# Undivided keys and queries for the first two units of an attention and expert kernel

## The chip, the cores and the metric

The kernel runs as one program on 1 core of a Trainium2 chip. The metric is the time of one execution on the device in microseconds (us); the median of several runs is compared. The engines are named as in the profile: PE is TensorE (PEld its weight loads), DVE is VectorE, ACT is ScalarE, POOL is GpSimd, and SP is the engine from whose queue nearly all transfers are issued.

## What is computed

Three layers run one after the other. The first is an attention that keeps, for each query, only the 32 largest scores:

```python
scores = scale * np.matmul(q, k.transpose(0, 1, 3, 2))      # 4 batches, 8 heads, 576 x 576, head_dim 64
kth = np.partition(scores, -top_k, axis=-1)[..., -top_k:-top_k + 1]    # top_k = 32
scores = np.where(scores >= kth, scores, -1e9)
attn = softmax(scores)
attn_out = np.matmul(attn, v)
```

Its output, as 2304 tokens of 512 numbers, goes through a feed-forward layer (`h = max(x @ w_in, 0); h * h @ w_out`, inner width 2048) and then through a layer of 8 experts (inner width 1024) of which a gate picks 2 for each token. All inputs are float32.

## The kernel before

**Division.** A float32 matrix is multiplied as a sum of products of two parts: a rounded one (`fp32r`, made by an ACT copy) and the remainder (a subtraction on DVE or POOL, in `split`, L398 to L401). For keys both parts lie in one tile: the head's 64 rows come twice in the input, rows 0 to 63 of `K4[b, g][:, h]` hold the rounded keys and rows 64 to 127 the remainder. `prep_k` (L403) loads keys into `kn` (2 buffers) and splits them; `prep_q` (L420) loads the queries of one tile and four heads into `qn` (2 buffers) and splits them into `qt[:, 0]` and `qt[:, 1]`. In batch 0 the first keys (`(b, g) == (0, 0)`, heads 0 to 3) come one head at a time and their remainder is made by DVE, as is that of the queries of the first tile; for all later ones it is made by POOL.

**Attention.** The work goes in units: one tile of 128 queries and one pair of heads (`pair_full`, 64 of them), and 16 smaller ones for the left-over 64 queries of each batch (`pair_left`). For each head of a unit `scores` (L429) issues four matmuls into the one `ps` buffer (two halves of the keys, two parts of the queries), ACT copies them to `sb` (L442), and DVE searches `sb`: five pieces of some 115 keys, each with MAX8 (L453) and MATCH_REPLACE8 (L457), and then a `threshold` (L479) that finds the 32nd largest. Its steps are interleaved with the pieces of the next head. The order of the search on DVE is fixed by tokens. Then POOL, ACT, POOL and ACT make the masked exponentials (L506 to L512), PE turns them (L523) and multiplies by the values (L564).

**Beside it.** While units run, `convert` (L144) makes the 32 parts of the feed-forward weights from their stored form: two ACT passes, two DVE passes (L155, L156) and one POOL pass (L158). The first 14 of them hold an intermediate in PSUM (`acc`), the other 18 in SBUF (`ca`). `zero_fill` writes zeros to two buffers in DRAM (`xs`, then `out`) from SP's queue. The feed-forward of tokens that are done is put between the units in small steps (`step`), at a pace that is set by sums of estimated costs; the first of its seven chunks runs in plain float32 (L315, L351).

**Order.** The code is written in the order of the units (L846 on: queries and keys of the first units, their scores, then `prep_k(0, 1, ...)`, values and the loop over units). A scheduler then orders the instructions of each engine by dependences, by priorities (`tc.high_priority`, `tc.cur_priority`) and by its own estimate of the times, so a change of a few instructions can move many others. An engine runs its own instructions strictly in that order.

**Lines that the prediction speaks of:** L400 and L401 (`split`), L409 (loads of keys), L424 (loads of queries), L439 (score matmuls), L442 (their copy), L453 (first search), L155 and L156 (conversion on DVE).

## Time and profile before

| | |
|---|---|
| median of 3 runs | 1337.8 us (1335.57 to 1337.93) |
| the profiled execution | 1336.86 us, of which its span is 1335.1 us |
| PE busy | 1241.5 us (93%) |
| DVE busy | 899.2 us (67%) |
| ACT busy | 856.6 us (64%) |
| POOL busy | 746.2 us (56%) |
| moved by DMA | 270.06 MB, mean 202 GB/s |

The span runs from the first to the last recorded instruction of the core. A busy share over the whole span mixes stages with different limits: the attention stage ends at about 760 us, and the experts fill the rest. So the share says little about one place; the views by stretch, the chain and the timelines do.

### The profile page before, as it was taken

What the parts mean: (1) busy time and instruction counts of PE and PEld (TensorE: products, weight loads), DVE (VectorE), ACT (ScalarE), POOL (GpSimd) and SP (SyncE); (2) the same over time, 40 slices, a digit from 0 to 9 for tenths busy, and PEclk for the clock granted to TensorE, in tenths of its full rate; (3) what the DMA queues carried; (4) which work ended last, traced back from release to release, by engine and by line L of the source; (5) the groups of instructions that cost most, each with busy time, mean ns of one, the idle gap of its engine ahead of it and who ended that gap; (6) DMA issues with size and microseconds to landing.
All of it is one profiled execution on the core that took longest, in us unless ns stands there. A gap on an engine that the chain in (4) does not pass through costs nothing.

```text
span 1335.1 us, 26136 instructions
## 1 busy us (share of the span) xinstructions
PE 1241.5 (93%) x8030; PEld 1071.8 (80%) x8030; DVE 899.2 (67%) x4557; ACT 856.6 (64%) x1886; POOL 746.2 (56%) x1243
## 2 busy tenths in 40 slices
PE   3769889989998999999999999999999999999997
PEld 2556667777887888888888888899899999988886
DVE  8999989998986899978677410255534343444554
ACT  6878879989897889987878653543433333332443
POOL 5857798887786676767655635333432241503221
PEclk9889999999999999999999999999999999999999
DMA  9998886875675554366534689366643443534464
GB/s 333 361 368 292 274 273 235 309 260 181 219 231 193 166 174 157 106 211 204 168 115 158 205 297 332 113 198 197 192 151 117 143 136 119 174 103 143 141 202 140
DMA packets 93302, 270.06 MB, mean 202 GB/s; under 512 B 11612, under 2 KB 11740, under 8 KB 93152
## 3 DMA queue, kind: packets, MB, share of 16 engines
q1 hardware_dynamic: 83872, 239.91, 54.3%
q0 software_dynamic: 9280, 28.40, 5.9%
q8 instruction: 65, 1.06, 0.3%
q14 instruction: 85, 0.70, 0.2%
HBM read 209.90 MB, written 60.45 MB: 202 GB/s over the span
## 4 chain that ended last, share of the span: by engine, by line
PE 61%; ACT 13%; DVE 11%; DMA 7%; issue 5%; POOL 3%; SPq 0%; POOLq 0%; DVEq 0%; ACTq 0%
PE pa L564 5%; PE ph L693 5%; PE ph L695 4%; PE ph L694 4%; PE acc L676 4%; PE acc L674 4%; PE acc L675 4%; PE ps L439 4%; PE pa L523 3%; PE acc L322 3%; PE acc L320 3%; PE acc L321 3%; DMA raww<-in_exp 3%; PE pf L357 2%; PE pf L358 2%
## 5 line engine op out<-in xcount | busy, mean ns | idle before, releaser
L511 POOL TENSOR_TENSOR sb<-sb,w 128x576 f32<-128x576 f32 x144 | 205.8, 1430 | 63.3 <-ACT w L510 59.3
L453 DVE MAX8 m<-sb 128x8 f32<-128x115 f32 (+1 forms) x720 | 190.3, 264 | 53.1 <-ACT sb L442 47.6
L457 DVE MATCH_REPLACE8 w<-m,sb 128x115 f32<-128x115 f32 (+1 forms) x720 | 187.1, 263 | 0.0
L699 ACT ACTIVATE ht<-ph 128x384 fp32r<-128x384 f32 (+1 forms) x128 | 55.8, 436 | 195.2 <-PE ph L695 177.0
L715 POOL DMA_INDIRECT out<-y,info x40 | 45.1, 1127 | 242.4 <-DVE y L714 224.7
L439 PE MATMUL ps<-K,qt 128*128 128x288 f32 (+2 forms) x640 | 131.4, 333 | 43.9 <-ACT sb L442 30.0
L700 DVE SCALAR_TENSOR_TENSOR ht<-ph,ht 128x384 fp32r<-128x384 f32 (+1 forms) x128 | 62.7, 490 | 161.7 <-ACT ht L699 148.5
L693 PE MATMUL ph<-xe,wi 128*128 128x256 f32 (+1 forms) x512 | 159.9, 312 | 1.9 <-ACT wi L686 1.0
L695 PE MATMUL ph<-xe,wi 128*128 128x256 f32 (+1 forms) x512 | 159.2, 311 | 0.2 <-DVE wi L687 0.2
L694 PE MATMUL ph<-xe,wi 128*128 128x256 f32 (+1 forms) x512 | 158.9, 310 | 0.0
L439 PEld LDWEIGHTS ps<-K,qt 128*128 128x128 f32 x640 | 103.7, 204 | 64.4 <-ACT sb L442 37.7
L512 ACT ACTIVATE sb<-sb,keep 128x576 f32<-128x576 f32 x144 | 112.5, 781 | 28.1 <-POOL sb L511 27.6
L674 PE MATMUL acc<-wo,ht 128*128 128x512 f32 x320 | 125.8, 397 | 0.4 <-DVE y L714 0.4
L675 PE MATMUL acc<-wo,ht 128*128 128x512 f32 x320 | 125.3, 395 | 0.0
L510 ACT ACTIVATE w<-sb,keep 128x576 f32<-128x576 f32 x144 | 111.3, 775 | 16.4 <-POOL keep L506 16.2
L371 POOL TENSOR_TENSOR gt<-r,gt 128x384 fp32r<-128x384 f32 (+1 forms) x96 | 90.7, 946 | 53.2 <-ACT gt L370 39.9
L481 DVE MAX8 m<-w 128x8 f32<-128x288 f32 x288 | 116.0, 443 | 0.1
L357 PE MATMUL pf<-xT,wi 128*128 128x384 f32 (+1 forms) x320 | 106.0, 331 | 5.4 <-ACT r L364 3.9
L523 PE MATMUL pa<-ident,sb 128*128 128x128 f32 x576 | 94.8, 289 | 16.5 <-ACT sb L512 7.1
L676 PE MATMUL acc<-wo,ht 128*128 128x512 f32 x320 | 108.9, 401 | 0.0
L525 ACT COPY pt<-pa 128x512 f32<-128x512 f32 x144 | 83.2, 578 | 32.1 <-PE pa L523 21.2
L693 PEld LDWEIGHTS ph<-xe,wi 128*128 128x128 f32 x512 | 96.4, 188 | 8.5 <-ACT wi L686 1.4
(211 smaller groups left out, 3511.9 us busy)
## 6 DMA issues: line engine op xcount, KB each, us to landing
raww<-in_exp SPq DMA_DIRECT2D x88, 512.0 KB
wi<-wsc SPq DMA_DIRECT2D x64, 512.0 KB
wo<-wsc SPq DMA_DIRECT2D x64, 512.0 KB
raw<-in_ffn SPq DMA_DIRECT2D x32, 512.0 KB
xs<-xr SPq DMA_DIRECT2D x40, 258.0 KB
mr<-xs SPq DMA_DIRECT2D x40, 258.0 KB
qn<-in_q SPq DMA_DIRECT2D x40, 256.0 KB
whole<-ca SPq DMA_DIRECT2D x32, 256.0 KB
```

Source lines behind the costliest of these rows:

```text
L357: nc.tensor.matmul(ph[:, 0:n], wi[:, 0, sl], xT[:, 0, c, 0:n], start=(c == 0), stop=False)
L439: nc.tensor.matmul(ps[:, n, 0:w], st, kt[:, at:at + w], start=(i == 0), stop=(i == len(pairs) - 1))
L453: in_turn(nc.vector.max(parts[i][1], sb[:, parts[i][0]]))
L457: in_turn(nc.vector.match_replace(out=w[:, sl], in_to_replace=top, in_values=sb[:, sl], imm_value=NEG))
L511: nc.gpsimd.tensor_tensor(sb, sb, w, op=ALU.subtract)
L523: nc.tensor.transpose(pt[:, c * P:(c + 1) * P], e[:, c * P:(c + 1) * P], ident)
L674: queued(nc.tensor.matmul(acc[t], hs[i][:, 0, sl], wo[:, 0, :], start=(f == 0), stop=False))
L675: queued(nc.tensor.matmul(acc[t], hs[i][:, 0, sl], wo[:, 1, :], start=False, stop=False))
L676: queued(nc.tensor.matmul(acc[t], hs[i][:, 1, sl], wo[:, 0, :], start=False, stop=(f == NFE - 1)))
L693: queued(nc.tensor.matmul(ph[:, 0:n], wi[:, 0, sl], xe[i][:, 0, c, :], start=(c == 0), stop=False))
L694: queued(nc.tensor.matmul(ph[:, 0:n], wi[:, 0, sl], xe[i][:, 1, c, :], start=False, stop=False))
L695: queued(nc.tensor.matmul(ph[:, 0:n], wi[:, 1, sl], xe[i][:, 0, c, :], start=False, stop=(c == NC - 1)))
```

## The change

The first two units (tile 0 of batch 0, heads 0 to 3) take their scores from `kn` and `qn` as loaded, in plain float32: one matmul per half of the keys instead of two, over 64 rows. As the head's rows lie twice in `kn` and `qn`, the first half of the keys uses rows 0 to 63 and the second half rows 64 to 127. The four heads share two `kn` buffers that stay in use until `divide_first`, which is called behind the scores of both units, has split them into `K4[0, 0]` for the later units. The remainders of these keys, and of the other queries of tile 0, are now made by POOL.

```diff
--- before.py
+++ after.py
@@ -404,12 +404,23 @@
 
         if j == 0:
             K4[b, g] = apool.tile([P, 4, S], F32R, name="K4", bufs=3)
-        for h in ([2 * j], [2 * j + 1]) if (b, g) == (0, 0) else ([2 * j, 2 * j + 1],):
-            kn = apool.tile([P, 2, S], F32, name="kn", bufs=2)[:, 0:len(h), :]
-            nc.sync.dma_start(kn, k[b, 4 * g + h[0]:4 * g + h[-1] + 1].rearrange("h p s -> p h s"))
-            dst = K4[b, g][:, h[0]:h[-1] + 1, :]
-            for i in range(len(h)):
-                split(nc.vector if (b, g) == (0, 0) else nc.gpsimd, dst[:, i], dst[:, i], kn[:, i], D)
+        kn = apool.tile([P, 2, S], F32, name="kn", bufs=2)
+        if (b, g) == (0, 0):
+            for i in range(2):
+                nc.sync.dma_start(kn[:, i, :], k[b, 2 * j + i])
+                undivided.append(kn[:, i, :])
+            return
+        nc.sync.dma_start(kn, k[b, 4 * g + 2 * j:4 * g + 2 * j + 2].rearrange("h p s -> p h s"))
+        for i in range(2):
+            dst = K4[b, g][:, 2 * j + i]
+            split(nc.gpsimd, dst, dst, kn[:, i], D)
+
+    undivided = []
+
+    def divide_first(j):
+        for h in (2 * j, 2 * j + 1):
+            dst = K4[0, 0][:, h]
+            split(nc.gpsimd, dst, dst, undivided[h], D)
 
     def prep_v(b):
         V[b] = []
@@ -422,11 +433,13 @@
 
         qn = apool.tile([P, 4, P], F32, name="qn", bufs=2)
         nc.sync.dma_start(qn.rearrange("p h s -> p (h s)"), q[b, s0 // P, g])
+        if (b, g, s0) == (0, 0, 0):
+            return qn
         qt = apool.tile([P, 2, 4, P], F32R, name="qt", bufs=3)
-        split(nc.vector if b == 0 and s0 == 0 else nc.gpsimd, qt[:, 0], qt[:, 1], qn, 0)
+        split(nc.gpsimd, qt[:, 0], qt[:, 1], qn, 0)
         return qt
 
-    def scores(pairs, sb, whole, then):
+    def scores(pairs, sb, whole, then, in_halves=False):
 
 
         ps = ps_s.tile([P, 2, 512], F32, name="ps")
@@ -436,7 +449,9 @@
                     at, w = n * HS, HS
                 else:
                     at, w = ((LEFT * par, NFULL * P), (0 if par else NFULL * P, LEFT))[n]
-                nc.tensor.matmul(ps[:, n, 0:w], st, kt[:, at:at + w], start=(i == 0), stop=(i == len(pairs) - 1))
+                rows = slice(n * D, (n + 1) * D) if in_halves else slice(0, P)
+                nc.tensor.matmul(ps[:, n, 0:w], st[rows], kt[rows, at:at + w], start=(i == 0),
+                                 stop=(i == len(pairs) - 1))
         with tc.high_priority(SOON):
             if whole:
                 nc.scalar.activation(sb.rearrange("p (n s) -> p n s", n=2), ps[:, :, 0:HS], AF.Copy)
@@ -565,17 +580,20 @@
                                              start=(n == 0), stop=(n == NFULL))]
         return av, t5[:, 1, :]
 
-    def pair_full(b, j, qt):
+    def pair_full(b, j, qt, keys=None):
 
         hA = 2 * j
         q0 = 2 * (j % 2)
         sm = apool.tile([P, 2], F32, name="sm", bufs=6)
         e = apool.tile([P, 2 * S], F32, name="sb", bufs=4)
         for i in range(2):
-            kt = K4[b, j // 2][:, (hA + i) % 4]
             sb = e[:, i * S:(i + 1) * S]
-            scores([(qt[:, 0, q0 + i, :], kt, i), (qt[:, 1, q0 + i, :], kt, i)], sb, True,
-                   lambda w, m, sb=sb, one=sm[:, i:i + 1]: softmax(sb, w, m, one))
+            if keys:
+                pairs = [(qt[:, q0 + i, :], keys[hA + i], i)]
+            else:
+                kt = K4[b, j // 2][:, (hA + i) % 4]
+                pairs = [(qt[:, 0, q0 + i, :], kt, i), (qt[:, 1, q0 + i, :], kt, i)]
+            scores(pairs, sb, True, lambda w, m, sb=sb, one=sm[:, i:i + 1]: softmax(sb, w, m, one), bool(keys))
             yield
         recip(sm)
         pts = [transpose4(e)]
@@ -811,6 +829,9 @@
 
     def start(i):
         b, s0, full, j, _ = units[i]
+        if i < 2:
+            gens[i] = pair_full(b, j, qtt[b, s0, j // 2], undivided)
+            return
         gens[i] = (pair_full if full else pair_left)(b, j, qtt[b, s0, j // 2])
 
     def close(i):
@@ -852,6 +873,8 @@
     start(1)
     next(gens[1])
     next(gens[1])
+    divide_first(0)
+    divide_first(1)
     prep_k(0, 1, 0)
     prep_k(0, 1, 1)
     prep_v(0)
```

How this moves instructions, at three places. On ACT at the start of the program (`K_...` is `K4[0, 0]`, `kn` the loaded keys, `sb` the copied scores of a head); before, then with the change:

```order
L400 ACTIVATE qt<-qn 128x512
L400 ACTIVATE K_120<-kn 128x576 x2
L442 ACTIVATE sb<-ps 128x576 x2
L400 ACTIVATE K_120<-kn 128x576 x2
L400 ACTIVATE qt<-qn 128x512 x2
L442 ACTIVATE sb<-ps 128x576
```

```order
L400 ACTIVATE K_117<-kn 128x576 x3
L457 ACTIVATE sb<-ps 128x576
L400 ACTIVATE K_117<-kn 128x576
L457 ACTIVATE sb<-ps 128x576
L400 ACTIVATE qt<-qn 128x512
L457 ACTIVATE sb<-ps 128x576
```

The copy of the first head's scores (L442, now L457) stood behind the query split and the key splits of two heads; it now stands behind the key splits of three heads.

On DVE, from the end of the first head's search on (L453 and L457 are now L468 and L472, L481 is L496, L484 is L499, L489 is L504); before, then with the change:

```order
L457 MATCH_REPLACE w<-m,sb 128x115 x2
L453 MAX m<-sb 128x8
L481 MAX m<-w 128x8 x2
L453 MAX m<-sb 128x8
L401 TENSOR_TENSOR K_120<-kn,K_120 64x576
L484 TENSOR_SCALAR low<-m 128x5x11
L457 MATCH_REPLACE w<-m,sb 128x116
L401 TENSOR_TENSOR K_120<-kn,K_120 64x576
L489 MAX low_164<-low 128x8
L453 MAX m<-sb 128x8
L401 TENSOR_TENSOR qt<-qn,qt 128x512
```

```order
L472 MATCH_REPLACE w<-m,sb 128x115 x2
L468 MAX m<-sb 128x8
L496 MAX m<-w 128x8 x2
L468 MAX m<-sb 128x8
L499 TENSOR_SCALAR low<-m 128x5x11
L472 MATCH_REPLACE w<-m,sb 128x116
L504 MAX low_152<-low 128x8
L468 MAX m<-sb 128x8
```

The three subtractions that stood between the steps of the search are gone from DVE, and three more that stood ahead of its first step.

On SP, which issues the transfers (`kn` keys, `vt` values, `qn` queries, `raw` weights, `xs` zeros); before, then with the change:

```order
L409 DMA kn<-in_k 128x576 x2
L418 DMA vt<-in_v 128x512 x5
L125 DMA wg<-in_route 128x64
L409 DMA kn<-in_k 128x576
L126 DMA nz<-in_noise 128x144
L409 DMA kn<-in_k 128x576
L424 DMA qn<-in_q 128x512 x2
L147 DMA raw<-in_ffn 128x1024 x4
L136 DMA xs<-xr 128x516 x4
L409 DMA kn<-in_k 128x2x576
L136 DMA xs<-xr 128x516
L409 DMA kn<-in_k 128x2x576
```

```order
L147 DMA raw<-in_ffn 128x1024 x4
L413 DMA kn<-in_k 128x2x576
L136 DMA xs<-xr 128x516 x5
L429 DMA vt<-in_v 128x512
L136 DMA xs<-xr 128x516 x2
L435 DMA qn<-in_q 128x512
L429 DMA vt<-in_v 128x512
L136 DMA xs<-xr 128x516 x2
L413 DMA kn<-in_k 128x2x576
```

With the change the four single-head loads stand together behind the first load of queries, ahead of the values. The keys of heads 4 and 5 (the first 128x2x576) now come right behind the four loads of weights; those of heads 6 and 7 (the second) behind nine loads of zeros instead of five.

## Rows read from the trace of the kernel before

**Rows 1.** The view by stretch, the whole core; its columns stand first.

```profile
core 0: us, PE busy (x) PEld busy (x) DVE busy (x) ACT busy (x) POOL busy (x), PEclk, DMA share, GB/s
6.00:7.00 1.00, 1.00 (x4) 0.76 (x4) 0.34 (x1) 0.63 (x1) 0.00 (x0) 1.00 1.07 358
8.00:192.00 184.00, 135.26 (x771) 100.16 (x772) 183.48 (x996) 149.82 (x320) 133.41 (x141) 0.91 0.95 327
192.00:430.00 238.00, 219.07 (x1713) 183.85 (x1712) 205.64 (x1313) 210.89 (x516) 195.35 (x301) 0.99 0.69 234
430.00:760.00 330.00, 322.15 (x2350) 282.70 (x2349) 268.04 (x1794) 272.14 (x618) 225.57 (x365) 1.00 0.50 164
760.00:1335.00 575.00, 563.50 (x3197) 503.91 (x3195) 239.06 (x448) 219.84 (x431) 188.58 (x410) 1.00 0.52 171
```

**Rows 2.** The chain in order of time, first 60 us; start, us, what.

```profile
1.24 3.00 DMA kn<-in_k
...
11.18 0.77 DVE K L401
...
12.24 0.21 issue
...
12.46 0.77 DVE K L401
...
13.64 0.59 DVE qt L401
...
56.58 2.33 PE pa L564 x20
```

**Rows 3.** The timeline of TensorE, first scores; start, us, line, op, count, [idle before <-releaser].

```profile
5.78 1.33 PE L439 MATMUL ps<-K,qt 128*128 128x288 f32 x4 [5.78 <-DVE K L401]
```

**Rows 4.** The timeline of ScalarE, copies and key splits.

```profile
4.26 0.68 ACT L400 ACTIVATE K<-kn 128x576 fp32r<-128x576 f32 x1
...
5.95 0.68 ACT L400 ACTIVATE K<-kn 128x576 fp32r<-128x576 f32 x1 [1.01 <-DMA kn<-in_k]
...
7.15 0.65 ACT L442 ACTIVATE sb<-ps 128x576 f32<-128x576 f32 x1 [0.52 <-PE ps L439]
...
26.38 1.26 ACT L400 ACTIVATE K<-kn 128x576 fp32r<-128x576 f32 x2 [0.94 <-DMA kn<-in_k]
```

**Rows 5.** The timeline of VectorE, first searches of four heads.

```profile
7.83 0.46 DVE L453 MAX8 m<-sb 128x8 f32<-128x116 f32 x2 [0.41 <-ACT sb L442]
...
9.97 0.27 DVE L453 MAX8 m<-sb 128x8 f32<-128x116 f32 x1
...
28.87 0.28 DVE L453 MAX8 m<-sb 128x8 f32<-128x116 f32 x1 [0.26 <-ACT sb L442]
...
36.51 0.27 DVE L453 MAX8 m<-sb 128x8 f32<-128x116 f32 x1
```

**Rows 6.** One line's instructions: plain float32 matmuls of L351; ns min/median/max.

```profile
L351 PE MATMUL pf<-xT,wi x128: 378/380/636, 102.2 to 199.1; 128*128 128x256 f32 x128
```

**Rows 7.** One line's instructions: plain float32 matmuls of L315; ns min/median/max.

```profile
L315 PE MATMUL acc<-wo,gt x64: 591/593/1062, 110.5 to 204.8; 128*128 128x512 f32 x64
```

**Rows 8.** The timeline of POOL, the first splits.

```profile
13.58 1.80 POOL L401 TENSOR_TENSOR qt<-qn,qt 128x512 fp32r<-128x512 f32 x1 [9.44 <-ACT qt L400]
...
26.76 4.16 POOL L401 TENSOR_TENSOR K<-kn,K 64x576 fp32r<-64x576 f32 x3
```

**Rows 9.** The waits of SP's queue, 0 to 60 us; in total, times, longest.

```profile
SPq L136 <- DMA xs<-xr: 9.4, 13, 1.7
```

**Rows 10.** One tile's instructions (ca), 0 to 230 us; ns min/median/max.

```profile
L155 DVE TENSOR_SCALAR ca<-ca x18: 400/590/1564, 112.4 to 180.5; 128x512 uint32<-128x512 uint32 x18
...
L156 DVE SCALAR_TENSOR_TENSOR ca<-raw,ca x18: 664/676/1896, 113.1 to 182.8; 128x512 uint32<-128x512 uint32 x18
```

**Rows 11.** Groups by line and shape, VectorE, 100 to 195 us.

```profile
L156 DVE SCALAR_TENSOR_TENSOR ca<-raw,ca 128x512 uint32<-128x512 uint32 x18 | 18.1, 1007 | 0.0
...
L155 DVE TENSOR_SCALAR ca<-ca 128x512 uint32<-128x512 uint32 x18 | 14.7, 818 | 0.0
```

## The prediction, made before the changed kernel ran

> **What bounds the kernel now.** I read the view by stretch first, to see which engine is full where. From 8 to 192 us DVE is busy for 183.48 of 184 us [rows 1]; PE has 135.26 there, ACT and POOL less than 150. So the search and the weight conversions on DVE set the pace of the first 192 us. From 192 us on PE takes over: 219.07 of 238, then 322.15 of 330, then 563.50 of 575 us [rows 1]. PE's work is fixed, and much of it (the feed-forward of tokens that are done) waits for what DVE has searched; so whatever DVE reaches earlier before 192 us should move the end by as much, and a gain of any other engine there moves nothing.
>
> Then I read the chain at its start, to see what stands ahead of DVE's search. It goes from the load of the first keys (3.00 us from 1.24 us [rows 2]) over ACT's and DVE's split and the score matmuls (5.78 us [rows 3]) to ACT's copy (7.15 us [rows 4]); the search begins at 7.83 us [rows 5] and DVE hardly rests again. Behind that, the chain lies on two key splits and a query split that DVE does in the midst of the search [rows 2].
>
> **Where the search begins.** The first score matmul no longer waits for splits, only for keys and queries: the keys land at 4.24 us (1.24 + 3.00 [rows 2]), so PE could begin some 1.5 us sooner than 5.78. What comes next on the path is not PE but ACT's queue. There the first head's copy now stands behind three key splits, and ACT takes its instructions in order. It can split head 0 at 4.26 and head 1 at 5.95 us, when that load lands [rows 4]. Head 2's load now follows head 1's: 288 KB are 0.295 MB, at 358 GB/s [rows 1] 0.82 us, so it lands at about 6.77. Then one split (0.68) and the copy (0.65 [rows 4]) end at 8.10, and the search begins at 8.12: **0.29 us later than before**. Lower bound: head 2 lands together with head 1, and the search begins at 7.98 (+0.15). Upper: it lands as long behind head 1 as that did behind head 0 (5.95 - 4.24 = 1.71), 7.66, and the search begins at 9.01 (+1.18). I take +0.29, by the rate of the queue at that time.
>
> **The second head.** DVE wants it 2.14 us after the first (9.97 - 7.83 [rows 5]). Its scores can start only when the one score buffer has been copied, so after the first copy come the matmuls (d), a copy of 0.65 and gaps of about 0.07: DVE waits for d - 1.42. Before, d was 1.33 us (four matmuls [rows 3]). Now it is two plain float32 matmuls of 288 columns. One such matmul is two records (128 records of L351 for 64 calls [rows 6]). From 256 to 512 columns a record grows from 636 to 1062 ns at its longest [rows 6, 7], 1.66 ns a column, so 0.48 us for 288. Four records in a row, the last with its tail (636 + 32 x 1.66 = 689 ns), take 3 x 0.48 + 0.69 = 2.13 us, and DVE would wait 0.71. If the two halves of the array work side by side it is 0.48 + 0.69 = 1.17, and no wait. The nearest row is L564: its plain float32 matmuls use half of the array's columns in turn, and 20 records of 128 columns take 2.33 us [rows 2], against 20 x 128 x 1.66 = 4.25 in a row, 0.55 of it. I take **no wait**, and keep 0.71 as the bound.
>
> The Trainium skill, "TensorEngine Tiling (Array Packing)", Key Properties, says that tiles operate independently and can load weights and multiply in parallel. By that rule the wait is nothing, and without it the sum below ends 0.71 us higher. The L564 rows agree for columns; no row of this trace shows row halves.
>
> **What DVE no longer does.** Behind the first search two key splits (0.77 each on the chain) and one query split (0.59) go, 2.13 us, with the gaps beside them (0.21 the largest [rows 2], about 0.28 in all): **2.41 us**. The three splits ahead of the first search were in the path of its start, which is counted above. Lead of DVE at this point: 2.41 - 0.29 = 2.12 us.
>
> **What takes that work.** POOL gets four key splits and a query split: 4 x 1.39 (4.16 for three) + 1.80 [rows 8] = 7.4 us. It was idle for 9.44 us before its first split [rows 8], and nothing on DVE waits for these results until the third unit's tile, so I cost it at nothing; if that cover were gone, the first maskings on POOL would be late by up to 7.4 us, with DVE still ahead in its own order. ACT has the same key splits and one query split less. SP issues as many loads. The loads of heads 2 and 3 now precede the values, so the second unit's keys are there long before the search wants them.
>
> **Units 3 and 4, the divided keys of heads 4 to 7.** They share `kn` with the undivided ones. Heads 4 and 5 now stand ahead of the zeros in the queue and come sooner; before, DVE waited 0.26 us for that unit [rows 5], and I take this wait as gone. Heads 6 and 7 come later. Ahead of their load stood 7794 KB (8 loads of 256 KB, four of 288, four weights of 512, five zeros of 258, the first pair's 576 and its own, 104 KB of small ones); now 9338 KB (10 of 256, nine zeros). The 1544 KB more are 1.58 MB, at 358 GB/s 4.4 us. They landed at 26.38 us [rows 4]; now 30.8. Then ACT's split (0.63) and POOL's (1.4) end at 32.8, four matmuls (1.33 [rows 3]) and the copy (0.65) at 34.8. DVE wanted this head at 36.51 [rows 5]; with the lead it wants it at 36.51 - 2.12 - 0.26 = 34.13. **It waits 0.7 us.** Lower bound: none, if the queue serves the pair out of order. Upper: the load waits behind one more slow block of zeros, for which SP waits up to 1.7 us [rows 9], 2.4 us in all.
>
> **The sum.** 2.12 + 0.26 - 0.7 = 1.7 us ahead after the fourth unit. From there DVE has work without a break to 192 us, and then PE has. So 1336.86 - 1.7 = 1335.2 us for the profiled execution (span 1335.1 plus 1.8 around it), which stands 0.9 us under the median of 1337.8; against the median **1336.1 us**. A measurement of this kernel can tell about 0.2%, 2.7 us, from no change, so this is "the same". With all bounds good the gain is 1.7 + 0.14 + 0.7 = 2.5; with all bad (0.89, 0.71, 1.7 more) the loss is 1.6.
>
> **The rivals.** The scheduler reorders about the first 430 us. The amounts of work between heads are nearly the same, yet the neighbours change, and one place is sensitive to that.
>
> *Fewer collisions (faster).* The 18 conversions that keep their intermediate in SBUF run between 112 and 183 us. Their DVE passes take 400 to 1564 and 664 to 1896 ns [rows 10], and in all 14.7 + 18.1 = 32.8 us [rows 11], where 18 x 0.40 + 18 x 0.664 = 19.2 would be the least. So 13.6 us are lost on DVE, while it is the bound. In the timeline 16 of the 36 passes are longer than their least by over 0.2 us, 0.85 us each. With five fewer stretched the gain is 4.2 more: 1331.9 us. For it: the order there changes, and chance sets who meets whom. The Trainium skill, "SBUF — State Buffer", Who interferes with whom, calls this an exclusive lock between DVE and GpSimd, which the later one to issue waits out; the passes of 1.5 us beside POOL passes of 1.3 us fit that.
>
> *More collisions (slower).* The same mechanism at the same place: two more stretched passes (1.7 us) eat the lead, and from the sixth on the kernel is slower by over 0.2%. With seven more it is 1336.1 + 5.9 = 1342.0 us.
>
> *Late keys (slower).* If heads 6 and 7 land 5 us behind the queue's estimate, DVE waits them out one for one: 1341.1 us. It decides from 4.4 us behind on, a landing at 35.2. Against it: SP's longest wait for a block of zeros in the first 60 us is 1.7 [rows 9], and it takes several in a row.
>
> That the change doesn't do what it says (an early first search) is already in the sum, through ACT's order. Were the copy not held up there, the search would begin 2 us sooner: 1334.1 us. The order of the rows excludes it.
>
> **How the numbers follow.** The forecast, with collisions about as before, 0.40, and all of it within 0.2%. Fewer collisions 0.36, faster. More collisions 0.17, slower. Late keys 0.07, of which 0.05 slower and 0.02 within 0.2%. So faster 0.36, same 0.42, slower 0.22. The forecast's own range is 1335.3 (gain 2.5) to 1339.4. The range of 8 in 10 takes in the collisions on both sides and, since PE idles 18.9 us between 192 and 430 us [rows 1] and a tenth of that may move either way, 1.9 us more: from 1331.9 - 1.9, with the best start 0.5 less, 1329.5, to 1342.0.
>
> **What would show it.** Right: first MAX8 at 8.0 to 9.0 us, behind ACT's third key split; no DVE subtraction of L401; fourth unit's first MAX8 at 34 to 35.5 us with a short wait on ACT's copy; DVE full to about 190 us; conversion passes between 28 and 37 us in all. Wrong: a first MAX8 before 7.8 us, DVE idle for microseconds before the fourth unit, or DVE's lead of the fourth unit lost or doubled before 192 us with the passes unchanged.

## The result, and the profile after

| | before | with the change |
|---|---|---|
| median of the runs | 1336.7 us of 4 (1335.57 to 1337.93) | 1345.88 us of 4 (1341.37 to 1349.33) |
| ratio, 95% interval | | 1.0065 [1.0047, 1.0083] |
| the profiled execution | 1336.86 us, span 1335.1 | 1341.37 us, span 1339.6 |

The kernel is **slower by 0.65%**, some 9 us, where 1336.1 us and a range of 1329.5 to 1342.0 had been predicted. The profiled execution is the fastest of the four and 4.5 us longer than that of before, so it shows about half of the loss.

Lines of the changed kernel: scores L453, their copy L457 (L459 for the left-over units), first search L468, threshold L499 to L509, masking L521 to L527, turning L538 and L565, a broadcast `rb` by POOL L563 and the matmul that wants it L566.

**The first 35 us came out close to the forecast.** The timeline of TensorE with the change, then its first four records by their line (ns min/median/max):

```profile
4.48 1.33 PE L453 MATMUL ps<-kn,qn 64*128 64x288 f32 x4 [4.48 <-DMA kn<-in_k]
...
32.68 1.33 PE L453 MATMUL ps<-K,qt 128*128 128x288 f32 x4 [1.26 <-POOL K L401]
```

```profile
L453 PE MATMUL ps<-kn,qn x4: 684/748/846, 4.5 to 5.1; 64*128 64x288 f32 x4
```

The timelines of ScalarE, VectorE and POOL with the change:

```profile
5.36 1.51 ACT L400 ACTIVATE K<-kn 128x576 fp32r<-128x576 f32 x2 [0.31 <-DMA kn<-in_k]
6.77 0.63 ACT L457 ACTIVATE sb<-ps 128x576 f32<-128x576 f32 x1
...
30.05 1.24 ACT L400 ACTIVATE K<-kn 128x576 fp32r<-128x576 f32 x2
```

```profile
7.43 0.46 DVE L468 MAX8 m<-sb 128x8 f32<-128x116 f32 x2 [4.06 <-ACT sb L457]
...
34.73 0.28 DVE L468 MAX8 m<-sb 128x8 f32<-128x116 f32 x1 [1.03 <-ACT sb L457]
```

```profile
5.19 5.50 POOL L401 TENSOR_TENSOR K<-kn,K 64x576 fp32r<-64x576 f32 x4 [1.06 <-ACT K L400]
...
31.22 2.78 POOL L401 TENSOR_TENSOR K<-kn,K 64x576 fp32r<-64x576 f32 x2 [0.34 <-POOL rb L563]
```

The score matmuls of a head take 1.33 us as before [rows 3]; the first records of the two halves start at 4.481 and 4.488 us, the second ones at 5.090 and 5.129. The first copy stands behind the third key split, as forecast, but the loads were there sooner, so the search begins at 7.43 us and not at 8.12. POOL does the key splits. DVE reaches the fourth unit at 34.73 us after a wait of 1.03; before, that was 36.51 [rows 5]: 1.78 us ahead.

**The loss comes later, in waits for copies.** The view by stretch with the change:

```profile
8.00:192.00 184.00, 135.16 (x758) 97.56 (x756) 177.18 (x978) 149.41 (x321) 137.66 (x148) 0.90 0.93 326
192.00:430.00 238.00, 217.71 (x1695) 184.62 (x1690) 204.95 (x1307) 207.91 (x503) 190.92 (x294) 0.98 0.68 232
430.00:760.00 330.00, 322.16 (x2364) 282.31 (x2364) 270.29 (x1813) 273.48 (x621) 228.32 (x367) 1.00 0.51 165
```

DVE is busy for 177.18 us where it was for 183.48 [rows 1]. Of the 6.3 us only some 2.2 are splits that it no longer does (0.76, 0.76 and 0.68) and 1.8 are shorter conversion passes (below); most of the rest is work that it reaches later (18 instructions fewer here, 19 more from 430 to 760 us). The waits of VectorE from 160 to 212 us, and from 270 to 400 (engine, line, waited for: us in total, times, longest), with the change, and its two longest on the timeline:

```profile
DVE m L468 <- ACT sb L459: 11.3, 2, 5.7
...
DVE m L468 <- ACT sb L457: 14.3, 5, 4.1
```

```profile
189.73 0.28 DVE L468 MAX8 m<-sb 128x8 f32<-128x116 f32 x1 [5.55 <-ACT sb L459]
...
199.63 0.28 DVE L468 MAX8 m<-sb 128x8 f32<-128x116 f32 x1 [5.73 <-ACT sb L459]
```

and the waits before:

```profile
DVE sm L518 <- ACT sm L517: 5.3, 3, 2.5
DVE m L453 <- ACT sb L444: 1.7, 1, 1.7
...
DVE m L453 <- ACT sb L442: 8.2, 5, 2.5
```

How far DVE is ahead can be read head by head: the start of a head's first threshold step (L484 before, L499 now; 144 heads) less its start in the kernel before, in us, negative is ahead. One profiled execution each; e1 to e18 are the experiments below (e10, e13 and e15, not in the table, stand at 6.9, 11.0 and 2.0 us at 440 us).

| head (us before) | change | e1 | e2 | e3 | e4 | e5 | e6 | e11 | e17 | e18 | e7 | e8 | e9 | e12 | e14 | e16 |
|---|---|---|---|---|---|---|---|---|---|---|---|---|---|---|---|---|
| 10 (58) | -1.6 | -0.3 | 3.2 | 1.2 | -1.5 | -1.5 | -0.2 | -1.5 | -0.9 | -1.6 | -0.7 | -0.7 | -0.8 | -0.7 | -1.2 | 0.1 |
| 31 (170) | -1.4 | -0.3 | 5.2 | -1.1 | -3.3 | -2.4 | -1.1 | -1.3 | 0.9 | 0.5 | 0.9 | -1.2 | -0.8 | 0.1 | 0.3 | -0.9 |
| 34 (189) | 2.1 | -0.3 | 8.7 | 0.1 | -2.2 | -2.4 | -1.1 | -1.3 | 0.9 | 0.5 | 4.4 | -1.2 | 5.7 | 2.1 | 3.8 | -0.9 |
| 46 (255) | 1.3 | -1.3 | 8.2 | 0.8 | -0.9 | -2.5 | -0.8 | -2.2 | 1.0 | -0.5 | 4.5 | -1.0 | 7.4 | 9.9 | 3.3 | -1.8 |
| 64 (348) | 7.4 | -1.3 | 18.4 | 4.5 | 2.7 | -2.5 | -0.1 | -2.2 | 1.7 | -0.5 | 4.6 | 4.6 | 7.3 | 10.1 | 10.6 | -1.7 |
| 82 (440) | 4.1 | -1.7 | 15.1 | 2.3 | 3.3 | -2.4 | -0.6 | -0.7 | 0.7 | -1.2 | 4.2 | 2.3 | 6.3 | 9.5 | 7.5 | -1.8 |

The lead of 1.6 us lasts to 170 us, is gone at 189, and DVE falls 7.4 us behind by 348. Some 3 us are made up by 440 us, and from there to 620 us the distance stays at 4.0 to 4.1.

**What stands there.** Of the instructions from the fifth unit to some 430 us that both orders hold (as the lists of e1 and e13 below have them), 259 of 467 on POOL, 507 of 780 on ACT and 788 of 1684 on DVE stand at another place of their queue, by up to 43 places. The copies of two left-over units, with the change and before:

```profile
175.25 0.58 ACT L459 ACTIVATE sb<-ps 128x512 f32<-128x512 f32 x1
...
189.10 0.60 ACT L459 ACTIVATE sb<-ps 128x512 f32<-128x512 f32 x1
```

```profile
172.20 0.60 ACT L444 ACTIVATE sb<-ps 128x512 f32<-128x512 f32 x1 [0.36 <-PE pa L550]
...
186.71 0.60 ACT L444 ACTIVATE sb<-ps 128x512 f32<-128x512 f32 x1
```

They come 3.05 and 2.39 us later than before, while DVE had got 3.8 us ahead just then (head 33); for the second it waits 5.55 us (189.73) and, one unit on, 5.73 (199.63).

**Collisions were not it.** The conversions with an intermediate in SBUF, by the tile's instructions with the change, sum to 14.9 and 16.1 us, 31.0 in all against 32.8 before [rows 11]:

```profile
L155 DVE TENSOR_SCALAR ca<-ca x18: 402/716/1516, 109.3 to 179.2; 128x512 uint32<-128x512 uint32 x18
L156 DVE SCALAR_TENSOR_TENSOR ca<-raw,ca x18: 665/677/1597, 111.2 to 180.4; 128x512 uint32<-128x512 uint32 x18
```

### The profile page after: what moved, and what is told of

It is laid out like the page before. It is cut to its first block, busy times and chain, and to the rows that moved or that the text cites. A ratio compares the mean times of both kernels' runs of the same rounds, so it can differ in the third digit from the quotient of the medians.

```text
span 1339.6 us, 26139 instructions
## 1 busy us (share of the span) xinstructions
PE 1244.7 (93%) x8030; PEld 1073.0 (80%) x8030; DVE 892.0 (67%) x4551; ACT 857.2 (64%) x1885; POOL 753.6 (56%) x1248
## 5 line engine op out<-in xcount | busy, mean ns | idle before, releaser
L468 DVE MAX8 m<-sb 128x8 f32<-128x115 f32 (+1 forms) x720 | 190.9, 265 | 71.9 <-ACT sb L457 56.5
L472 DVE MATCH_REPLACE8 w<-m,sb 128x115 f32<-128x115 f32 (+1 forms) x720 | 187.5, 263 | 0.0
L453 PE MATMUL ps<-K,qt 128*128 128x288 f32 (+1 forms) x624 | 127.9, 330 | 32.5 <-ACT sb L457 25.1
L453 PEld LDWEIGHTS ps<-K,qt 128*128 128x128 f32 x624 | 99.6, 199 | 51.7 <-ACT sb L457 32.0
L527 ACT ACTIVATE sb<-sb,keep 128x576 f32<-128x576 f32 x144 | 112.2, 779 | 29.0 <-POOL sb L526 28.5
L525 ACT ACTIVATE w<-sb,keep 128x576 f32<-128x576 f32 x144 | 111.3, 774 | 20.1 <-POOL keep L521 20.0
L496 DVE MAX8 m<-w 128x8 f32<-128x288 f32 x288 | 116.0, 444 | 0.1
L538 PE MATMUL pa<-ident,sb 128*128 128x128 f32 x576 | 94.4, 288 | 15.4 <-ACT sb L527 7.7
L357 PE MATMUL pf<-xT,wi 128*128 128x384 f32 (+1 forms) x320 | 105.5, 330 | 3.2 <-ACT r L364 3.2
L359 PE MATMUL pf<-xT,wi 128*128 128x384 f32 (+1 forms) x320 | 102.4, 320 | 1.8 <-POOL wi L341 1.8
```

The costliest lines, as they stand in the source:

```text
L453: nc.tensor.matmul(ps[:, n, 0:w], st[rows], kt[rows, at:at + w], start=(i == 0), stop=(i == len(pairs) - 1))
L468: in_turn(nc.vector.max(parts[i][1], sb[:, parts[i][0]]))
L472: in_turn(nc.vector.match_replace(out=w[:, sl], in_to_replace=top, in_values=sb[:, sl], imm_value=NEG))
L496: in_turn(nc.vector.max(m[:, 40 + 8 * i:48 + 8 * i], w[:, i::2]))
L527: nc.scalar.activation(sb, sb, AF.Exp, bias=bs[:, 3:4] if keep is not None else bs[:, 0:1], scale=SCALE, accum_out=sm)
```

## The experiments

Theory: the change gains what was forecast, and the order that the scheduler draws for the other instructions of the first 430 us loses more. Rival: the change costs by itself, through POOL's new work or the later keys.

### Change and order apart (e1, e2)

Each engine got a list of instruction numbers and a dependence without a semaphore from each entry to the next, so that the scheduler keeps that order from the fifth unit to some 430 us:

```diff
+    by_name = {i.name: i for i in nc.cur_bb.bb.instructions}
+    for ids in json.loads(zlib.decompress(base64.b85decode(ORDER))).values():
+        for a, b in zip(ids, ids[1:]):
+            tc.add_manual_dep(by_name[f"I-{b}"], f"I-{a}", ...)
```

e1 is the changed kernel in the old order, e2 the kernel before in the new one.

> The changed kernel, with the order of the kernel before written in by hand (as dependences that only fix the issue order) on all five engines, from the fifth unit on, to past 430 us. Theory O (the change itself gains 1.7 us by the fifth unit; what it loses later comes only from the order that the scheduler redraws from there to 430 us): 1.0 to 2.5 us under the kernel before, about 1335 us, with the lead of VectorE kept to 430 us. Rival C (the change costs by itself, by the splits that POOL now does and the work that it displaces): slower than before by 4 us or more, about as the changed kernel.

> The kernel before, unchanged in its work, with the order of the changed kernel written in on all five engines from the fifth unit on. Theory O: slower than the kernel before by 5 to 11 us (the 4 to 9 that the changed kernel shows, and the lead of 1.7 that it lacks), 1342 to 1348 us. Rival C: within 2.7 us of the kernel before, since its work is unchanged.

e1: 1334.57 us against 1334.81, ratio 1.0001 [0.9987, 1.0015]. e2: 1345.99 us, ratio 1.0081 [1.0056, 1.0105]. **The order alone makes the loss**: with all of the old work and none of the change it costs 0.8%. The two waits at the left-over units are there to the hundredth, as VectorE's timeline of e2 shows:

```profile
196.36 0.28 DVE L609 MAX8 m<-sb 128x8 f32<-128x116 f32 x1 [5.55 <-ACT sb L600]
...
206.27 0.28 DVE L609 MAX8 m<-sb 128x8 f32<-128x116 f32 x1 [5.73 <-ACT sb L600]
```

That a written list costs by itself is excluded by e16 below, the kernel before with its own order as a list and one move: ratio 0.9999 [0.9990, 1.0009]. How large the loss is, is known less well: the same new order gives 0.65% in the changed kernel (4 runs), 0.81 in e2 (4 runs) and 0.39 [0.24, 0.54] in e13 (9 runs, below). The change in the old order costs nothing, but gains nothing that these runs can tell. Why, VectorE's and ScalarE's timelines of e1 show:

```profile
46.53 0.70 DVE L311 TENSOR_SCALAR acc<-acc 128x512 uint32<-128x512 uint32 x1 [1.88 <-ACT acc L309]
```

```profile
41.02 0.78 ACT L681 ACTIVATE w<-sb,keep 128x576 f32<-128x576 f32 x1 [0.87 <-POOL keep L677]
```

POOL, with five more splits ahead, is late with a mask; ACT waits for it, its conversion pass stands behind, and DVE waits 1.88 us for that in the midst of the search. 1.4 of the 1.7 us are gone at 58 us, by this one trace. The old order was drawn for a POOL without these splits.

### Another small edit, another draw (e3, e4)

In e3 (the kernel before) and e4 (the changed one) DVE does the first step of the first two heads twice, some 0.5 us; the second result is dropped.

```diff
+                    for _ in range(1 if i == 0 and not searched[0] and not pending else 0):
+                        in_turn(nc.vector.max(parts[i][1], sb[:, parts[i][0]]))
```

> The kernel before with the first MAX8 of each of the first two heads done twice (the same result; 2 x 0.18 us more on VectorE), which makes the scheduler redraw its order up to about 430 us, as the change does. Theory O: the time moves by several us, in either direction, by far more than the 0.4 us of added work; a move of 2 to 10 us in size. Rival C: 0.4 us slower, within 0.2%.

> The changed kernel with the same two repeated MAX8, and an order redrawn once more. Theory O: the time moves away from that of the changed kernel by several us, in either direction, and may fall below the kernel before. Rival C: 0.4 us over the changed kernel, 6 to 12 us over the kernel before.

e3: 1336.67 us, ratio 1.0015 [1.0002, 1.0028]; e4: 1341.33 us, ratio 1.0045 [1.0028, 1.0061]. In e3's trace, matched by kind and turn, some 280 of POOL's 467 instructions stand at another place because of two added on DVE. Of its 0.15% the work is 0.04. These two runs do not part theory and rival: e3's 1.9 us are fewer than the 2 to 10 of the theory and within the rival's 0.2%, and e4's interval overlaps that of the changed kernel. What the theory rests on is e2. A new draw cost between 0.1 and 0.8% here; none of those seen was better than the old one.

### The new order for 60 us, the old behind (e5)

Two lists can be joined at any time of a run: what an engine had begun by then stands in the one order, the rest in the other. e5 leaves the change its own order to 61 us, made with POOL's splits in view, and takes the old one from there.

> The change; every engine's instructions stand in the order of the changed kernel for its first 61 us and from there in the order of the kernel before. The first run with the old order lost 1.4 us of the lead at 46 us to a wait on ACT; here DVE should be about 1.7 us ahead of the kernel before at 70 us. Theory carried (what DVE gains before 192 us moves the end): the lead stays 1.5 to 1.8 us to the left-over units at 180 us and the end; span 1.4 us under that of the run with the old order, median about 1333.2, ratio to before 0.9988. Rival absorbed (PE and the waits between 192 and 430 us take it up): the lead is there at 170 us and is what the run with the old order had (1.65) or less at 440 us; median about 1334.6, ratio 1.000.

1332.27 us against 1335.25, ratio 0.9986 [0.9972, 1.0000]; span 1330.3 against e1's 1332.3. The lead is 1.5 us at 58 us and 2.4 at 440. This speaks for *carried*: the early lead reaches the end where the order behind does not lose it. It is not shown: the intervals of e1 and e5 overlap, their traces were taken on different chips, and among the runs within 2.5 us the lead of one execution does not order the ratios (at 440 us e1 is 1.7 ahead with a ratio of 1.0001, e11, further down, 0.7 ahead with 0.9984).

### Earlier still (e6, e11)

e6 moves four things in e5's lists:

```diff
 ACT:  key split head 0
+      copy of the first head's scores
       key splits heads 1 to 3
...
       copy of the scores of head 5
+      key splits heads 6, 7
 SP:   load of keys 4, 5
+      load of keys 6, 7
 POOL: product x2
+      key splits heads 6, 7
       query split, mask, rb
```

> As the run beside it, and in the first 60 us three more places are moved by hand: the copy of the first head's scores right behind the first key split on ACT, the load of the keys of heads 6 and 7 right behind that of heads 4 and 5, and their splits ahead of the next query split. First MAX8 at about 6.5 us instead of 7.4, no wait of DVE at the fourth unit's first head (1.03 before): up to 1.9 us more lead at 60 us. Theory carried: the whole of it shows at the end, span 3.3 us under that of the kernel before and below, median 1331.5 to 1333, ratio 0.9975. Rival absorbed: lead of up to 3.6 us at 170 us, no more than 1.7 at the end, ratio 0.9985 to 1.000.

1334.67 us, ratio 1.0001 [0.9990, 1.0012], a miss. The search begins at 6.44 us, but the lead at 58 us is 0.2. TensorE's timeline of e6:

```profile
33.96 0.48 PE L734 MATMUL pa<-ident,rb 128*128 128x128 f32 x1 [2.09 <-POOL rb L731]
34.09 1.31 PE L621 MATMUL ps<-K,qt 128*128 128x288 f32 x4
```

The fourth unit's keys are ready earlier, but its score matmuls stand on PE behind the matmul that wants `rb`, and `rb` now stands on POOL behind the key splits and a query split: PE waits 2.09 us. On ACT the third head's copy (12.45) stands behind a query split that waits 3.22 us for its load. e11 mends both: that copy ahead of that split, and on POOL the mask and `rb` between the two key splits.

> Second try at an earlier start on top of the new order to 60 us and the old behind. The first try lost what it won because ACT's copy of the third head stood behind a query split that waited for its load, and because POOL's key splits held back the broadcast that PE waits for. Here the third head's copy stands ahead of that query split, and on POOL the broadcast stands between the two key splits and the query splits behind them. Theory carried: first MAX8 at 6.4 us, no wait over 0.3 us at the fourth unit's first head, lead over the kernel before of 2.5 to 3.5 us at 70 us (1.76 without these moves), all of it at the end: median 1330.5 to 1331.5 against 1332.3. Rival (another wait takes its place in the first 60 us, as in the first try): lead below 1.8, median 1332.3 or more.

1334.89 us against 1336.98, ratio 0.9984 [0.9972, 0.9996]. The search begins at 6.50 us and the fourth unit has no wait, and yet that unit begins at 34.70, no sooner than with the change alone (34.73): 0.68 us go in a wait at the second head, 0.76 at a normalisation that waits for ACT, and the rest to other work. The lead at 58 us is e5's (at 440 us 0.7 are left of it), and so is the time, within the intervals. So the rival holds for the moves, and e5 and e11 are **the versions that beat both kernels**, by some 0.15%; e11's interval lies wholly below 1, e5's ends there.

### Which stretch of the order (e7, e8, e17, e18)

New order to 250 us and the old behind (e7), the mirror (e8), and the joint of e7 at 118 (e17) and at 160 us (e18):

> The change in its own order to 250 us, from there in the order of the kernel before. DVE is then late by what it lost at 189 us: +0.3 to +1.2 us between 212 and 250 us as in the changed kernel. Theory late order (most of the loss is made by the order between 250 and 430 us, where DVE waits on ACT copies that stand behind late work): no further loss, DVE +0.5 to +1.5 at 440 us, median 1335.5 to 1337, ratio 1.001. Rival early order (what is set up before 250 us makes the loss): DVE +4 at 440 us, median 1341 or more, ratio 1.005.

> The mirror: the change in the order of the kernel before to 250 us, from there in its own. DVE is 1.3 us ahead at 250 us. Theory late order: it loses some 4 to 7 us between 280 and 350 us, and is +2 to +4 at 440 us; median 1339 to 1342, ratio 1.003 to 1.005. Rival early order: no loss there, median about 1334.6, ratio 1.000.

> The change in its own order to 118 us, in that of the kernel before from there; the same joint lay at 61 us in the run that gained (ratio 0.9986) and at 250 us in the one that lost (1.0028). Theory early (what loses is set up between 61 and 118 us, where DVE's lead goes from 1.6 us to nothing): DVE behind by 1 us or more at 189 us and at 440 us, ratio 1.0005 to 1.0020. Theory late (the order behind 118 us): no wait of DVE over 3 us at 190 us, lead of 1 us or more at 440 us, ratio 0.9980 to 1.0000.

> The same with the joint at 160 us, behind PE's wait for the broadcast and its half clock, ahead of the key splits of the next batch. Theory splits (the order of POOL's splits and of the left-over units from 160 us on makes the two waits of 5.5 us): DVE waits below 3 us at 190 us and is ahead at 212 us, ratio 0.9985 to 1.0005. Theory PE (it is late by what happened before 160 us): waits of 3 us or more at 190 to 200 us, DVE behind at 212 us by 1 us or more, ratio 1.0010 to 1.0030.

| | new order from .. to | us | ratio |
|---|---|---|---|
| e5 | 0 to 61 | 1332.27 | 0.9986 [0.9972, 1.0000] |
| e17 | 0 to 118 | 1335.61 | 0.9996 [0.9983, 1.0009] |
| e18 | 0 to 160 | 1334.91 | 0.9995 [0.9983, 1.0007] |
| e7 | 0 to 250 | 1338.66 | 1.0028 [1.0015, 1.0042] |
| e8 | 250 to 430 | 1339.48 | 1.0039 [1.0024, 1.0053] |

VectorE's timeline of e18, then of e7, then of e8:

```profile
197.73 0.28 DVE L635 MAX8 m<-sb 128x8 f32<-128x116 f32 x1 [1.42 <-ACT sb L626]
```

```profile
192.09 0.28 DVE L635 MAX8 m<-sb 128x8 f32<-128x116 f32 x1 [5.55 <-ACT sb L626]
...
201.99 0.28 DVE L635 MAX8 m<-sb 128x8 f32<-128x116 f32 x1 [5.73 <-ACT sb L626]
```

```profile
299.73 0.28 DVE L628 MAX8 m<-sb 128x8 f32<-128x116 f32 x1 [4.22 <-ACT sb L617]
...
316.67 0.28 DVE L628 MAX8 m<-sb 128x8 f32<-128x116 f32 x1 [3.17 <-ACT sb L617]
```

**Two stretches lose: 160 to 250 us and 250 to 430 us.** With the joint at 250 us the two waits of the changed kernel are there to the hundredth (5.55, 5.73); with the joint at 160 they are gone. e8 goes from 1.0 us ahead at 255 us to 4.6 behind at 348, with waits like those of the changed kernel there (4.22 and 3.17, against 4.13 and 3.17). Between 61 and 160 us the new order may lose 1 to 3 us of what e5 won (e17 and e18 against e5 at 440 us), but single executions of one order differ by some 2 us as well (e7 and the change at 170 us). Two expectations failed in part: e7 was to be at +0.5 to +1.5 at 440 us and is at 4.2, because what DVE is late at 189 us is carried too; and e17 fits neither of its theories (0.9 us behind at 189 us, no wait over 3 us there, ratio 0.9996).

### What makes the copy at 190 us late (e9, e12, e13 to e16)

On ACT that copy stands behind four masking passes that wait for POOL, and PE has its scores since some 182 us. e9 is e7 with the copy (L459, L460) taken ahead of them, from 191.5 us in e7 to behind a copy at 184.0.

> The kernel with the new order to 250 us and the old one behind, and one pair moved on ACT: the copy of the first left-over unit's scores that DVE awaits at 189.7 us (5.55 us of waiting) is taken ahead of four masking passes that stand behind POOL's key splits; PE has had these scores ready since some 180 us. Theory in-order queue (ACT's copy only waits its turn behind passes that wait for POOL): DVE's wait of 5.5 us there falls to below 1.5, DVE stands some 4 us better at 200 us than in the run without the move, and at least 2.5 us of it are left at 440 us: median 1334.5 to 1336.5 against 1338.7. Rival backlog (POOL's and ACT's work of that stretch is late as such; the copy only shows it): the wait turns up again at the next heads before 212 us, DVE gains less than 1 us at 212 us, median 1338 to 1339.

1343.57 us, ratio 1.0066 [1.0047, 1.0085], worse than theory and rival had it. ScalarE's timeline of e9:

```profile
189.23 0.60 ACT L626 ACTIVATE sb<-ps 128x512 f32<-128x512 f32 x1 [5.12 <-PE pa L732]
```

Its place in the queue was not what held it: the copy waits 5.12 us for PE to turn an older unit (L732 is L565), which frees one of the four `sb` buffers, and now the masking passes wait behind it. e12 starts at the other end: POOL's second pair of key splits of batch 1 and a query split go behind the masked products of that stretch, and one masking pass on ACT is taken earlier.

```diff
 POOL: conversion
-      key splits x2 (batch 1, heads 2 and 3)
       mask
-      query split
       xT, conversion, rb, mask, product, conversion, xT, mask, product x2
+      key splits x2, query split
```

> The kernel with the new order to 250 us and the old one behind, as the run in which the copy was moved; the copy is back in its place. That run showed the copy waiting 5.1 us for PE's turning of an older unit, which frees one of the four score buffers, so the copy was not held by its place in ACT's queue. Here POOL's second pair of key splits of batch 1 and its query split (some 5 us, 175.5 to 180.7 us) are moved behind the masked products of that stretch, and the masking pass on ACT that waits for them stands three conversions earlier. Theory POOL's order (what is late is the chain mask on POOL, exponential on ACT, product on POOL, turning on PE, and it is late by the splits ahead of it): DVE's wait of 5.55 us at 192 us falls by 2.5 us or more, DVE stands at +2 or better at 212 us where it was +2.6 with an unlucky start of 0.9 at 170 us, that is 1.5 us or more gained between 170 and 212 us; median 1335.5 to 1337.5. Rival (POOL is full there in any order): the wait stays over 4 us or its place is taken by another before 212 us; median 1338 to 1340.

1348.69 us, ratio 1.0105 [1.0088, 1.0122]. VectorE's, SP's and TensorE's timelines of e12:

```profile
189.71 0.28 DVE L635 MAX8 m<-sb 128x8 f32<-128x116 f32 x1 [4.51 <-ACT sb L626]
208.37 0.28 DVE L635 MAX8 m<-sb 128x8 f32<-128x116 f32 x1 [14.49 <-ACT sb L626]
```

```profile
191.87 0.38 SPq L580 DMA_DIRECT2D kn<-in_k  x1
...
194.61 0.38 SPq L500 DMA_DIRECT2D wo<-whole  x1
```

```profile
200.22 3.49 PE L482 MATMUL acc<-wo,gt 128*128 128x512 f32 x4 [6.60 <-DMA wo<-whole]
```

The first wait shrinks by 1.0 us, less than half of what was expected, and the time is far over both forecasts. Then POOL frees the key buffer only at 191.8 us, the next load of keys holds SP's queue until 191.87 (181.39 in e7), the two loads of weights `wo` behind it go out at 194.61 and 196.97 instead of 186.15 and 189.69, PE waits 6.60 us for one with a turning behind, and DVE waits 14.49.

A third suspect stands 60 us ahead: in the changed kernel, e2, e7, e9, e12 and e13 PE waits 2.71 to 2.73 us for one `rb` at 128 to 134 us, and in the changed kernel the granted clock is then half (last section). e14 takes the reciprocal on DVE and `rb` on POOL sooner, in the full new order; e13 is that order with nothing moved; e15 is the move in e7's lists; e16 is the mirror, the kernel before in its own order with that `rb` taken behind xT, a mask and a conversion.

> The changed kernel with its own order written down as a list, nothing moved: the measure for the next run. Same as the changed kernel: median 1341 to 1346, ratio 1.0045 to 1.0080; PE waits 2.7 us at some 128 us for POOL's broadcast rb and has half its clock for 6 us behind that.

> The same list with one broadcast taken sooner at 127 us: on DVE the reciprocal ahead of three search steps and a conversion pass, on POOL the broadcast rb made from it ahead of a masked product, a mask and nothing else. In every kernel with the new order PE stands 2.71 to 2.73 us at the matmul that wants this broadcast (0.25 in the order before), and from then on its granted clock is 0.50 for some 6 us, so that it is 3 to 4 us late with the feed-forward and the turnings up to 190 us. Theory PE (this late PE is what makes the copy at 190 us late, and PE's lost time is what reaches the end): the wait is below 0.5 us, no half clock at 130 to 136 us, DVE's wait at 190 us falls from 5.5 to 3.5 us or less, and the median is 2 to 4 us below that of the kept list. Rival chain (POOL's masks and products set the copy at 190 us, PE's wait is beside it): the wait at 128 us goes, the one at 190 us stays over 4.5, median within 1 us of the kept list. Rival gate (PE is gated soon after in another place): the wait goes and half clock turns up elsewhere before 190 us; median within 1.5 us.

> The same two moves in the list that has the new order to 250 us and the old one behind (which gave 1338.66 us, ratio 1.0028). Theory PE: DVE gains 2 us or more against that run between 170 and 255 us, ratio 1.0000 to 1.0010. Rivals: ratio 1.0022 to 1.0035.

> The mirror: the kernel before, its own order written down, with the one broadcast taken later on POOL, behind the next copy of the tokens, a mask and a conversion (some 3 us). Theory PE: PE waits 2.5 to 3 us at 129 us, has half its clock for some 6 us behind it, DVE waits at the copies at 185 to 200 us 2 to 3 us more than before, and the kernel is 2 to 4 us slower, ratio 1.0015 to 1.0030. Rivals: PE's wait is there, the copies and the end do not move, ratio 0.9995 to 1.0010.

| | us | ratio |
|---|---|---|
| e13 new order, kept | 1342.76 | 1.0039 [1.0024, 1.0054] |
| e14 `rb` sooner | 1344.49 | 1.0050 [1.0031, 1.0068] |
| e15 `rb` sooner, old order from 250 us | 1341.42 | 1.0025 [1.0011, 1.0039] |
| e16 before, `rb` later | 1336.88 | 0.9999 [0.9990, 1.0009] |

TensorE's timeline of e14, then of e16:

```profile
134.21 3.78 PE L511 MATMUL pf<-xT,wi 128*128 128x256 f32 x8 [4.15 <-ACT r L524]
```

```profile
132.50 0.47 PE L708 MATMUL pa<-ident,rb 128*128 128x128 f32 x1 [3.17 <-POOL rb L705]
```

e13, the changed kernel's order as a list, was to come to 1.0045 to 1.0080 and came out just below that.

Taken away, the wait is replaced by one of 4.15 us for ACT with half clock behind it (3.78 us for eight matmuls), and DVE still waits 5.56 us at 191 us. Added to the kernel before (3.17 us, granted clock 0.72 and 0.85 in the two stretches of 8 us behind it), it costs nothing: PE is full from 136 to 152 us and idles again behind that. And e18, with the joint at 160 us, has this wait as well (2.72 us at 132 us) without the loss. So this wait is **not the cause**, and the theory of a late PE, as e14 put it, falls with it.

### The scatter at 290 us (e10)

In e8 POOL's four indirect transfers (L272, 289.7 to 295.1 us) stand ahead of a masked product for which ACT waits; e10 spreads them from 300 to 308 us.

> The kernel with the old order to 250 us and the new one behind, and one thing moved on POOL: the four indirect transfers of the scatter (some 5.4 us, 289.7 to 295.1 us), which stand ahead of a masked exponential there, are taken behind two of them, spread from 300 to 308 us. Theory in-order queue: the copy that DVE awaits at 299.7 us (4.22 us) stands behind ACT passes that wait for POOL's product; with the transfers gone from there the wait falls by 2 to 4 us, and DVE stands 2 us better at 316 us than in the run without the move; part of it may be lost where the transfers now stand. Median 1336.5 to 1338.5 against 1339.5. Rival (the loss of 280 to 350 us lies in PE's or DVE's order): the wait stays over 3 us, median 1339 to 1340.

1342.12 us, ratio 1.0040 [1.0020, 1.0061], e8's. The wait behind them fell from 4.22 to 2.87 us and the next rose from 3.17 to 4.20; at 348 us DVE is 8.5 us behind, where e8 is 4.6. Neither forecast held. Inconclusive.

## Why the prediction was wrong

**The step that failed** is in the sum: "From there DVE has work without a break to 192 us, and then PE has." The lead of 1.7 us was to be carried to the end by engines that are full. In the old order that may hold (e5). The change gave the kernel another order for 430 us, in which DVE has no work for 5.55 us at 190 us and for 4.13 at 302. The prediction knew of the reordering, but let it act at one place only ("one place is sensitive to that"), the stretched conversions, and priced its slower rival there; for the rest of the order it put 1.9 us into its range, and at the lower end only (the upper end, 1342.0, is the collisions alone). e2 shows what the order is worth: +0.81% [0.56, 1.05], some 11 us (5 us by e13). The sign that the prediction gave for being wrong is what came: the lead lost before 192 us, with the conversion passes hardly changed.

Point by point:

- **Start of the search:** forecast +0.29 us, measured -0.40 (7.43 against 7.83). The mechanism was right (copy behind three key splits); the terms mis-sized were two loads. The second head's split was put at 5.95 us and began at 5.36; the third head's load was put at 6.77 us by the queue's rate, when its split was all but done and the copy began.
- **Second head:** no wait from its scores, as forecast. The row halves run side by side: their first records start 7 ns apart and last 813 and 846 ns, and all four take 1.33 us, against 2.13 worked out for four in a row and 1.17 for this case. The rule of tiles that work independently and in parallel (the Trainium skill, "TensorEngine Tiling (Array Packing)", Key Properties) agrees with the row.
- **Fourth unit:** forecast 34 to 35.5 us with a wait of 0.7; measured 34.73 with 1.03. Lead 1.78, forecast 1.7. That they agree is partly luck: the search began 0.69 us sooner than in the sum, the wait is 0.33 longer, and some 0.3 more went in between.
- **POOL's splits, costed at nothing:** wrong in the old order (e1 loses 1.4 us at 46 us through a late mask), right in the new one.
- **The lead carried:** not refuted where the order allows it; e5 gains 1.9 us by its ratio [0, 3.7], the sum gave 1.7, and e1 gains nothing that can be told.
- **Collisions:** neither rival; 31.0 us, within the 28 to 37 given. **Late keys:** no. ACT split them at 30.05 us without a wait for the load, which had been put at 30.8; the 1.03 us above are the way from there, over POOL's split (31.22 us) and the score matmuls, which waited 1.26 us for it.

**What stays open:** which moved instruction in 160 to 250 us and in 250 to 430 us does it. Five runs with single moves (e9, e10, e12, e14, e15) took one wait away and got another in its place or left it; only whole stretches of the order, put back, took the loss away. And about half of the 9 us is outside the profiled execution. The other three runs of the changed kernel have spans of 1343.4 to 1347.6 us at a mean granted clock of 0.976 to 0.979, against 0.980; where they lost it is not known, as they have no trace.

## What to carry to other kernels

Where a scheduler orders the queues, a change of a few instructions is two changes: its work, and a new order for hundreds of instructions that have nothing to do with it. Price them apart: give the order a range of its own (here up to 0.8%, to the slower side, since the order that was kept may be a lucky one), and write the old order down as a list to measure the work alone. If the work gains, keep its own order where it acts and the old one behind, as e5 does. And a wait names only the last link of a chain through in-order queues, buffers and loads: moving that link mostly moves the wait.

## What the runs showed of the hardware

**A wait of PE can be followed by half its clock.** TensorE's stretches with the change (us, PE busy, granted clock, DMA share, GB/s), then its timeline there, then that of the kernel before:

```profile
128.00:130.00 2.00, 0.00 (x0) 1.00 0.89 293
130.00:132.00 2.00, 1.13 (x3) 0.51 0.52 186
132.00:134.00 2.00, 2.00 (x6) 0.50 0.69 188
134.00:136.00 2.00, 2.00 (x7) 0.50 0.64 229
136.00:138.00 2.00, 2.00 (x24) 0.78 0.80 239
```

```profile
130.41 0.48 PE L566 MATMUL pa<-ident,rb 128*128 128x128 f32 x1 [2.71 <-POOL rb L563]
131.35 3.78 PE L351 MATMUL pf<-xT,wi 128*128 128x256 f32 x8 [0.46 <-ACT r L364]
```

```profile
130.16 2.00 PE L351 MATMUL pf<-xT,wi 128*128 128x256 f32 x8 [0.40 <-ACT r L364]
```

Behind a wait of 2.71 us the granted clock is 0.50, the lower of PE's two levels (1.2 instead of 2.4 GHz), for some 6 us, and eight matmuls take 3.78 us instead of 2.00 in the kernel before, where it is 1.00 from 130 to 132 us. Split by PE's idle time and what it lost to the lower clock (summed over stretches of 2 us, busy time times one less the granted clock), the spans read:

| | PE idle, us | lost to the clock, us | span, us | rest |
|---|---|---|---|---|
| before | 93.7 | 16.0 | 1335.1 | 1225.4 |
| change | 94.9 | 20.1 | 1339.6 | 1224.6 |
| e2 | 102.4 | 22.1 | 1348.9 | 1224.4 |
| e5 | 89.9 | 17.3 | 1330.3 | 1223.1 |
| e16 | 95.1 | 15.0 | 1335.5 | 1225.4 |

The rest, PE's work, is the same within some 2 us. So in the profiled execution most of the 4.5 us stands under PE's clock (+4.1), and 1.2 under the waits themselves, with 0.8 less rest; the stretch from 128 to 192 us has +2.8 of the clock's part and that from 270 to 350 us +3.2, and the others give 1.9 back. This is an account of where the time stands, not of its cause: e16 has half clock behind its added wait too (0.60 from 132 to 140 us), and yet PE loses no more to the clock in all, since stretches at half clock that the kernel before has at 156, 186 and 364 us are not there.
